# Low-part products of the last 64 gating tokens as 64-row matmul pairs

## The chip, the cores and the metric

The kernel runs on one core of one Trainium2 chip. The metric is the device time of one execution in microseconds (us); where several executions were timed, their median is given.

## The reference

Three layers follow one another: attention with rotary positions, a gated layer that mixes tokens, and a layer with a short convolution as gate. Shapes: batch 4, 8 heads of 64, 576 tokens, model width 512. The change is in the second layer:

```python
h = gelu_tanh(x @ w_in)                      # x (4, 576, 512), w_in (512, 1024)
u, v = h[..., :512], h[..., 512:]
v_n = (v - mean(v)) / sqrt(var(v) + 1e-6) * g_ln
v_s = einsum('ts,bsd->btd', w_sg, v_n) + b_sg[None, :, None]   # w_sg (576, 576)
x2  = x + (u * v_s) @ w_out
```

The sum over the 576 tokens s of `w_sg[t, s] * v_n[s, d]` is what the change touches.

## The kernel before

All matmuls outside the products with v and the sums of attention are made of parts: each number is split into a high part (rounded to a shorter type) and a low part (the rest), and a product is the sum of high x high, high x low and low x high, each a matmul in the shorter type.

In the gating, a *unit* computes 128 of the 512 features d for all 576 queries t: its accumulators are two halves of 288 queries, `ps[:, 0]` and `ps[:, 1]`, in two banks. The 576 tokens s are four chunks of 128 and a rest of 64. For the four chunks a unit runs 3 matmuls each per half of the queries (line 724). The rest has only 64 rows, so it is doubled up: a tile `T4` of 128 rows holds the high part of the 64 tokens in rows 0 to 63 and their low part in rows 64 to 127, and the chunk 4 of the weights holds the same 64 rows twice (lines 338 and 339), high parts in `SG[0]` and low parts in `SG[1]`. A matmul of the whole of `T4` with `SG[0]` therefore adds high x high and low x high; one with `SG[1]` adds high x low and low x low (line 727). So a unit is 2 x (12 + 2) = 28 matmuls, and there are four units for each of four batches.

`T4` is written by ScalarE twice from the normalized values (lines 696 and 697: the high part, into rows 64 to 127 and into rows 0 to 63), and then GpSimd subtracts the high part from the values and puts the low part into rows 64 to 127 (lines 699, 700; in the profile the tile is called `t`, and the subtraction has the line of its helper, 250).

After its last matmul VectorE reads a unit's accumulators, scales and adds the bias (line 731), GpSimd multiplies with u, and the result goes to memory. Four accumulator tiles take turns.

The order of the work on all engines is not written by hand. Each step is added to a plan with an engine, an estimated cost (`PASS` = 0.132 us a matmul of 288 columns) and the keys that it reads and writes; the plan works out due times and lays the steps out one after the other, each engine in its own queue. TensorE's steps keep the order in which they were added. A batch adds the products for v (line 671), those for u (line 710) and then the four gating units.

Other lines that are named below are of the attention stage: line 418 (scores for the maximum, two matmuls of 64 rows, one for each of two heads), line 426 (the same for the last 64 keys' queries, 128 rows), line 464 (transposed scores, four pairs of 64-row matmuls), line 472 (the rest of the keys, eight matmuls of 128 rows), line 495 (products with v, 128 rows and 64 columns). Line 789 is the first product of the last stage.

Of the kernel before, what the change touches and what calls it, by code (L numbers as in the profile page):

```python
# [26 lines left out]
class Plan:  # L27
# [6 lines left out]
    def add(self, eng, cost, fn, r=(), w=(), after=(), lat=0.0, lock=False, kb=0.0):  # L34
        k = len(self.tasks)
        deps = set(after)
        for key in r:
            deps.update(self.writer.get(key, ()))
        for key in w:
            deps.update(self.writer.get(key, ()))  # L40
            deps.update(self.readers.get(key, ()))
        for key in r:
            self.readers.setdefault(key, []).append(k)
        for key in w:
            self.writer[key] = [k]
            self.readers[key] = []
        if eng == "PE":
            if self.last_pe is not None:
                deps.add(self.last_pe)
            self.last_pe = k  # L50
        deps.discard(k)
        self.tasks.append((eng, cost, fn, tuple(sorted(deps)), lat, lock, (tuple(w) or tuple(r))[0:1]))
        self.kb.append(kb)
        return k
# [95 lines left out]
def act(n):  # L150
    return 0.11 + 0.833e-3 * n
# [15 lines left out]
def mixer_kernel(ctx: ExitStack, tc: tile.TileContext, qk, v, vrem, cs, w_in, g_ln, w_sgT, b_sg,  # L167
# [78 lines left out]
    def tt(e, out_, a, b, op, n, r, w):  # L246

        if e == "D":
            return add("DVE", dve(n), lambda: nc.vector.tensor_tensor(out_(), a(), b(), op), r, w, lock=True)  # L249
        return add("Pool", pool(n), lambda: nc.gpsimd.tensor_tensor(out_(), a(), b(), op), r, w, lock=True)  # L250
# [407 lines left out]
    def part_a(b):  # L658
        X, Wm, SG = (XH, XL), (w_h, w_l), (s_h, s_l)
        VN, T4, U, GL, VS, ST = (lambda n=n: T[n] for n in ("vn", "t4", "u", "gl", "vs", "st"))  # L660
        hl = "hl"
        xk = [("X", k, m) for k in range(4) for m in hl]
        for c0 in (0, 2, 4):
            cs_ = (c0, c0 + 1) if c0 < 4 else (4,)

            def mm(ps, cs_=cs_):
                for y, c in enumerate(cs_):
                    o = 128 * c if c < 4 else S - 128
                    for k in range(4):
                        for z, (p, q) in enumerate(three(3)):  # L670
                            nc.tensor.matmul(ps[:, y], X[p][:, k, o:o + 128], Wm[q][:, k, 512:1024], start=k == z == 0,  # L671
                                             stop=k == 3 and z == 2)
            ps, kp = unit(12 * 0.233 * len(cs_), mm, [*xk, *[(f"win{k}_1", m) for k in range(4) for m in hl]])
            gi = c0 // 2 % 2
            kg = ("gl", gi)
            n2 = len(cs_)
            add("Act", act(512 * n2), lambda ps=ps, gi=gi, n2=n2: nc.scalar.activation(
                GL()[gi][:, 0:n2], ps[:, 0:n2], AF.Gelu_apprx_tanh), [kp], [kg])
            for y, c in enumerate(cs_):
                kst = ("st", c % 3)  # L680

                def st(c=c):
                    return ST()[c % 3]
                add("DVE", dve(512), lambda st=st, gi=gi, y=y: nc.vector.bn_stats(st()[:, 0:6], GL()[gi][:, y]), [kg], [kst])
                add("DVE", 0.12, lambda st=st: nc.vector.bn_aggr(st()[:, 6:8], st()[:, 0:6]), w=[kst])
                add("DVE", 0.12, lambda st=st: nc.vector.tensor_scalar(st()[:, 8:9], st()[:, 7:8], 1e-6, None, ALU.add), w=[kst])
                add("Pool", 0.6, lambda st=st: nc.gpsimd.tensor_tensor(st()[:, 9:10], st()[:, 8:9], mhalf, ALU.pow),
                    [("consts",)], [kst])
                add("DVE", 0.46, lambda st=st, gi=gi, y=y: nc.vector.tensor_scalar(
                    GL()[gi][:, y], GL()[gi][:, y], st()[:, 6:7], st()[:, 9:10], ALU.subtract, ALU.mult), [kst, kg],  # L690
                    [("gl", gi, y)], lock=True)
                if c < 4:
                    split(lambda c=c: VN()[0][:, c], lambda c=c: VN()[1][:, c], lambda gi=gi, y=y: GL()[gi][:, y], DM,
                          [("gl", gi, y), kg], ("vn", c, "h"), ("vn", c, "l"))
                else:
                    add("Act", 2 * act(512), lambda gi=gi: (nc.scalar.copy(T4()[0][64:128], GL()[gi][64:128, 0]),
                                                            nc.scalar.copy(T4()[0][0:64], GL()[gi][64:128, 0])),
                        [("gl", gi, y), kg], [("vn", 4, "h")])
                    tt("P", lambda: T4()[0][64:128], lambda gi=gi: GL()[gi][64:128, 0], lambda: T4()[0][64:128].bitcast(F32),
                       ALU.subtract, 512, [("gl", gi, y), kg, ("vn", 4, "h")], [("vn", 4, "l")])  # L700

        def u_unit(dd):
            dc = slice(128 * dd, 128 * dd + 128)

            def mm(ps):
                for hf in range(2):
                    cols = slice(HALF * hf, HALF * hf + HALF)
                    for k in range(4):
                        for z, (p, q) in enumerate(three(3)):
                            nc.tensor.matmul(ps[:, hf, 0:HALF], Wm[p][:, k, dc], X[q][:, k, cols], start=k == z == 0,  # L710
                                             stop=k == 3 and z == 2)
            ps, kp = unit(24 * PASS, mm, [*xk, *[(f"win{k}_0", m) for k in range(4) for m in hl]])
            add("Act", act(S), lambda: nc.scalar.activation(U()[0][:, dd], ps[:, :, 0:HALF], AF.Gelu_apprx_tanh), [kp],
                [("u", dd)])

        def g_unit(dd):
            dc = slice(128 * dd, 128 * dd + 128)

            def mm(ps):
                for hf in range(2):  # L720
                    cols = slice(HALF * hf, HALF * hf + HALF)
                    for k in range(4):
                        for z, (p, q) in enumerate(three(3)):
                            nc.tensor.matmul(ps[:, hf, 0:HALF], VN()[p][:, k, dc], SG[q][:, k, cols], start=k == z == 0,  # L724
                                             stop=False)
                    for z in range(2):
                        nc.tensor.matmul(ps[:, hf, 0:HALF], T4()[0][:, dc], SG[z][:, 4, cols], start=False, stop=z == 1)  # L727
            ps, kp = unit(28 * PASS, mm, [("vn", c, m) for c in range(5) for m in hl] + [("sg", c, m) for c in range(5) for m in hl])
            y = dd % 2
            kv = ("vs", y)  # L730
            add("DVE", dve(S), lambda: nc.vector.scalar_tensor_tensor(
                VS()[y], ps[:, :, 0:HALF], gsb[:, dd:dd + 1], bsb, ALU.mult, ALU.add), [kp, ("gsb",), ("bsb",)], [kv])
            tt("P", lambda: VS()[y], lambda: VS()[y], lambda: U()[0][:, dd], ALU.mult, S, [("u", dd)], [kv])
            dma(290, lambda q: q.dma_start(out=g_d[b][dc, :], in_=VS()[y].rearrange("p a b -> p (a b)")), [kv],
                [("g_d", b, dd)])

        for dd in range(4):
            u_unit(dd)
        if b + 1 < B:
            x_prep(b + 1)  # L740
        for dd in range(4):
            g_unit(dd)
# [129 lines left out]
    def close_att():  # L872
        stT.close()
        p1 = ctx.enter_context(tc.tile_pool(name="pB1", side="right", bufs=1))
        for nm in "ovq":
            T["wh" + nm] = p1.tile([128, 4, DM], F32R, name=f"wh_{nm}")
            T["wl" + nm] = p1.tile([128, 4, DM], F32R, name=f"wl_{nm}")
        T["gh"] = [p1.tile([128, 4, S], F32R, name="gh0"), XH]
        T["gl_"] = [p1.tile([128, 4, S], F32R, name="gl0"), XL]
        pa2 = stA2.enter_context(tc.tile_pool(name="pA2", side="right", bufs=1))  # L880
        T["vn"] = [pa2.tile([128, 4, DM], F32R, name=f"vn{j}") for j in range(2)]
        T["t4"] = [pa2.tile([128, DM], F32R, name="t4")]
        T["u"] = [pa2.tile([128, 4, S], F32, name="u")]
        T["gl"] = [pa2.tile([128, 2, 512], F32, name=f"gl_{j}") for j in range(2)]
        T["vs"] = [pa2.tile([128, 2, HALF], F32, name=f"vs{j}") for j in range(2)]
        T["st"] = [pa2.tile([128, 12], F32, name=f"st{j}") for j in range(3)]
# [108 lines left out]
```

## Time and profile before

| | |
|---|---|
| median of 3 runs | 607.65 us (605.95 to 608.03) |
| profiled execution | 606.36 us |
| its span, first to last instruction | 604.6 us |
| mean granted TensorE clock | 0.986 of full |
| TensorE matmul busy | 586.5 us, 97% of the span |
| TensorE weight load (PEld) busy | 472.0 us, 78% |
| VectorE / ScalarE / GpSimd busy | 392.6 / 276.4 / 299.0 us |

In the rows of the trace PE is TensorE's matmuls and PEld its weight loads, which can overlap matmuls. An operation is written as line, operation, output<-inputs, then for TensorE the rows*columns of the array that it uses and the shape of its moving operand. Matmuls overlap in the pipeline, so the duration of one is longer than the step from its start to the start of the next. "x2" at one line joins two instructions. What stands in brackets is idle time before an instruction and what ended it; "issue" means that the engine waited for nothing that the profile shows.

### The profile page before, as it was taken

What the parts mean: (1) busy time and instruction counts of PE and PEld (TensorE: products, weight loads), DVE (VectorE), ACT (ScalarE), POOL (GpSimd) and SP (SyncE); (2) the same over time, 40 slices, a digit from 0 to 9 for tenths busy, and PEclk for the clock granted to TensorE, in tenths of its full rate; (3) what the DMA queues carried; (4) which work ended last, traced back from release to release, by engine and by line L of the source; (5) the groups of instructions that cost most, each with busy time, mean ns of one, the idle gap of its engine ahead of it and who ended that gap; (6) DMA issues with size and microseconds to landing.
All of it is one profiled execution on the core that took longest, in us unless ns stands there. A gap on an engine that the chain in (4) does not pass through costs nothing.

```text
span 604.6 us, 12082 instructions
## 1 busy us (share of the span) xinstructions
PE 586.5 (97%) x4682; PEld 472.0 (78%) x4682; DVE 392.6 (65%) x584; ACT 276.4 (46%) x448; POOL 299.0 (49%) x239
## 2 busy tenths in 40 slices
PE   7769999999999999999999999999999999999996
PEld 4546666666666666666898998998999989999995
DVE  6576777676666676654656865565397898837730
ACT  2336555556555656565542532523516454333321
POOL 5556666566555554456677846665455222201200
PEclk9679999999999999999999999999999999999999
DMA  6623555454455623666438347162433242130102
GB/s 221 205 79 91 149 165 145 126 127 126 121 128 132 188 53 91 192 192 174 139 122 298 118 149 235 47 204 91 145 116 99 60 137 92 39 127 2 36 27 95
DMA packets 55274, 76.81 MB, mean 127 GB/s; under 512 B 26544, under 2 KB 31152, under 8 KB 55216
## 3 DMA queue, kind: packets, MB, share of 16 engines
q1 hardware_dynamic: 54992, 76.03, 41.6%
q8 instruction: 37, 0.61, 0.4%
q14 instruction: 21, 0.17, 0.1%
q10 hardware_dynamic: 224, 0.00, 0.0%
HBM read 55.33 MB, written 18.95 MB: 123 GB/s over the span
## 4 chain that ended last, share of the span: by engine, by line
PE 86%; DVE 8%; issue 1%; DMA 1%; POOL 1%; ACT 0%; SPq 0%; ACTq 0%; DVEq 0%; POOLq 0%
PE ps L495 11%; PE ps L464 10%; PE ps L671 9%; PE ps L822 8%; PE ps L789 8%; PE ps L724 8%; PE ps L851 8%; PE ps L710 7%; PE ps L418 5%; DVE raw L249 4%; PE ps L472 3%; PE ps L531 3%; DVE mx L420 3%; PE ps L505 2%; PE ps L727 1%
## 5 line engine op out<-in xcount | busy, mean ns | idle before, releaser
L420 DVE TENSOR_REDUCE mx<-ps 128x2 f32<-128x576 f32 x128 | 96.4, 757 | 69.0 <-PE ps L418 68.5
L477 ACT ACTIVATE e<-ps 128x576 f32<-128x576 f32 x144 | 87.3, 649 | 77.1 <-PE ps L464 50.2
L495 PE MATMUL ps<-e,vm 128*64 128x288 f32 x512 | 78.3, 428 | 0.9 <-DVE mx L420 0.9
L250 POOL TENSOR_TENSOR ac<-e,e 128x576 f32<-128x576 f32 x32 | 50.5, 1600 | 40.3 <-PE ps L531 33.8
L724 PE MATMUL ps<-s_h,vn 128*128 128x288 f32 x256 | 56.1, 295 | 0.0
L249 DVE TENSOR_TENSOR raw<-raw,cst 128x576 f32<-128x576 f32 (+1 forms) x63 | 52.2, 857 | 6.0 <-DMA cst<-cs 6.0
L418 PE MATMUL ps<-kh,qp 64*128 64x288 f32 x256 | 49.4, 384 | 5.7 <-ACT qp L253 2.7
L418 PEld LDWEIGHTS ps<-kh,qp 64*128 64x128 f32 x256 | 25.0, 191 | 38.3 <-DVE mx L420 13.4
L250 POOL TENSOR_TENSOR raw<-raw 128x576 f32<-128x576 f32 x29 | 41.3, 1430 | 26.4 <-DVE raw L249 26.3
L495 PEld LDWEIGHTS ps<-e,vm 128*64 128x64 f32 x512 | 31.6, 138 | 24.2 <-issue 6.9
L724 PEld LDWEIGHTS ps<-s_h,vn 128*128 128x128 f32 x256 | 42.8, 188 | 0.1
L464 PE MATMUL ps<-qh,kh 64*128 64x288 f32 x256 | 41.1, 315 | 0.0
L464 PE MATMUL ps<-mr,one_r 64*128 64x288 f32 x256 | 39.3, 299 | 1.2 <-DMA mr<-mn 1.2
L464 PE MATMUL ps<-ql,kh 64*128 64x288 f32 x256 | 38.8, 297 | 0.4 <-DVE ql L249 0.4
L464 PE MATMUL ps<-qh,kl 64*128 64x288 f32 x256 | 38.6, 296 | 0.0
L822 PE MATMUL ps<-xh,wh_v 128*128 128x288 f32 x128 | 37.8, 295 | 0.0
L710 PE MATMUL ps<-XH,w_l 128*128 128x288 f32 x128 | 37.8, 295 | 0.0
L822 PE MATMUL ps<-xh,wl_v 128*128 128x288 f32 x128 | 37.8, 295 | 0.0
L724 PE MATMUL ps<-s_l,vn 128*128 128x288 f32 x128 | 37.8, 295 | 0.0
L822 PE MATMUL ps<-xl,wh_v 128*128 128x288 f32 x128 | 37.8, 295 | 0.0
L710 PE MATMUL ps<-XL,w_h 128*128 128x288 f32 x128 | 37.8, 295 | 0.0
L710 PE MATMUL ps<-XH,w_h 128*128 128x288 f32 x128 | 37.7, 295 | 0.0
(155 smaller groups left out, 1594.4 us busy)
## 6 DMA issues: line engine op xcount, KB each, us to landing
raw<-qk SPq DMA_DIRECT2D x31, 576.0 KB, 4.4
xu_d<-xu SPq DMA_DIRECT2D x32, 144.0 KB, 2.8
rb<-r_d SPq DMA_DIRECT2D x32, 144.0 KB, 3.3
xs<-xu_d SPq DMA_DIRECT2D x16, 288.0 KB, 4.0
x_d<-xs SPq DMA_DIRECT2D x16, 288.0 KB, 3.0
g_d<-vs SPq DMA_DIRECT2D x16, 288.0 KB, 3.3
vm<-v SPq DMA_DIRECT2D x16, 256.0 KB, 3.3
wr<-w_in SPq DMA_DIRECT2D x8, 512.0 KB, 5.2
```

The costliest lines, as they stand in the source:

```text
L249: return add("DVE", dve(n), lambda: nc.vector.tensor_tensor(out_(), a(), b(), op), r, w, lock=True)
L250: return add("Pool", pool(n), lambda: nc.gpsimd.tensor_tensor(out_(), a(), b(), op), r, w, lock=True)
L418: nc.tensor.matmul(ps[:, h, 0:HALF], QP[j2][rows, c], kh[rows, cols], start=True, stop=True)
L420: add("DVE", 0.76, lambda: nc.vector.tensor_reduce(out=MX[j2][:, hk, :, c], in_=ps[:, :, 0:HALF], axis=AX.X, op=ALU.max), [kps], [("mx", j ...
L464: nc.tensor.matmul(ps[:, h, 0:HALF], x[rows, keys] if o < 3 else x[rows], y[rows, cols], start=o == 0, stop=o == 3)
L477: add("Act", 0.62, lambda: nc.scalar.activation(E[n], ps[:, :, 0:HALF], AF.Exp), [kps], [("e", n)])
L495: nc.tensor.matmul(pv[64 * hf:64 * hf + 64, h, 0:HALF], VM[j2][:, j, h], E[EU[i, us[hf]]][:, h], start=j == 0, stop=False, skip_group_chec ...
L671: nc.tensor.matmul(ps[:, y], X[p][:, k, o:o + 128], Wm[q][:, k, 512:1024], start=k == z == 0, stop=k == 3 and z == 2)
L710: nc.tensor.matmul(ps[:, hf, 0:HALF], Wm[p][:, k, dc], X[q][:, k, cols], start=k == z == 0, stop=k == 3 and z == 2)
L724: nc.tensor.matmul(ps[:, hf, 0:HALF], VN()[p][:, k, dc], SG[q][:, k, cols], start=k == z == 0, stop=False)
L789: nc.tensor.matmul(ps[:, hf, 0:HALF], w2("o", p)[:, k, dc], (T["gh"], T["gl_"])[q][j][:, k, cols], start=k == z == 0, stop=k == 3 and z == 2)
L822: nc.tensor.matmul(ps[:, hf, 0:HALF], w2("v", p)[:, k, dc], (T["xh2"], T["xl2"])[q][j][:, k, cols], start=k == z == 0, stop=k == 3 and z == 2)
```

## The change

Of each unit, the matmuls of `T4` with the low parts of the weights (two, one per half of the queries, 128 rows each) are replaced by two of 64 rows: rows 0 to 63 for the first half of the queries, and rows 64 to 127 for the second half, issued one behind the other at the end of the unit. The low x low product falls away. For the second one the high part is needed in rows 64 to 127 as well, so there is a second tile `T4()[1]`: the first of the two ScalarE copies goes to its rows 64 to 127, and GpSimd's subtraction reads the high part from there and writes the low part to `T4()[0]` as before. The plan's cost of a unit is 27 passes in place of 28.

```diff
-                    add("Act", 2 * act(512), lambda gi=gi: (nc.scalar.copy(T4()[0][64:128], GL()[gi][64:128, 0]),
+                    add("Act", 2 * act(512), lambda gi=gi: (nc.scalar.copy(T4()[1][64:128], GL()[gi][64:128, 0]),
                                                             nc.scalar.copy(T4()[0][0:64], GL()[gi][64:128, 0])),
                         [("gl", gi, y), kg], [("vn", 4, "h")])
-                    tt("P", lambda: T4()[0][64:128], lambda gi=gi: GL()[gi][64:128, 0], lambda: T4()[0][64:128].bitcast(F32),
+                    tt("P", lambda: T4()[0][64:128], lambda gi=gi: GL()[gi][64:128, 0], lambda: T4()[1][64:128].bitcast(F32),
                        ALU.subtract, 512, [("gl", gi, y), kg, ("vn", 4, "h")], [("vn", 4, "l")])
...
-                    for z in range(2):
-                        nc.tensor.matmul(ps[:, hf, 0:HALF], T4()[0][:, dc], SG[z][:, 4, cols], start=False, stop=z == 1)
-            ps, kp = unit(28 * PASS, mm, [("vn", c, m) for c in range(5) for m in hl] + [("sg", c, m) for c in range(5) for m in hl])
+                    nc.tensor.matmul(ps[:, hf, 0:HALF], T4()[0][:, dc], SG[0][:, 4, cols], start=False, stop=False)
+
+                for hf in range(2):
+                    rows = slice(64 * hf, 64 * hf + 64)
+                    nc.tensor.matmul(ps[:, hf, 0:HALF], T4()[hf][rows, dc], SG[1][rows, 4, HALF * hf:HALF * hf + HALF],
+                                     start=False, stop=True)
+            ps, kp = unit(27 * PASS, mm, [("vn", c, m) for c in range(5) for m in hl] + [("sg", c, m) for c in range(5) for m in hl])
...
-        T["t4"] = [pa2.tile([128, DM], F32R, name="t4")]
+        T["t4"] = [pa2.tile([128, DM], F32R, name=f"t4_{j}") for j in range(2)]
```

## Rows read from the trace of the kernel before

**Rows 1.** The page: busy time by engine, and the chain that ended last by engine.
```profile
PE 586.5 (97%) x4682; PEld 472.0 (78%) x4682; DVE 392.6 (65%) x584; ACT 276.4 (46%) x448; POOL 299.0 (49%) x239
...
PE 86%; DVE 8%; issue 1%; DMA 1%; POOL 1%; ACT 0%; SPq 0%; ACTq 0%; DVEq 0%; POOLq 0%
```
**Rows 2.** Windows: gating units of batch 1, and the last stage; columns in the first line.
```profile
core 0: us, PE busy (x) PEld busy (x) DVE busy (x) ACT busy (x) POOL busy (x), PEclk, DMA share, GB/s
...
351.10:365.93 14.83, 14.83 (x114) 14.83 (x113) 9.43 (x11) 3.22 (x6) 9.32 (x6) 1.00 0.66 205
...
448.90:604.60 155.70, 151.10 (x985) 142.03 (x983) 103.49 (x142) 59.82 (x101) 31.59 (x18) 1.00 0.22 73
```
**Rows 3.** Chain in order of time, batch 1's gating: start, us, what.
```profile
351.10 1.60 PE ps L724 x12
352.70 0.27 PE ps L727 x2
...
365.93 0.23 PE ps L671
```
**Rows 4.** What TensorE's matmuls waited for, 311 us to the end: total, times, longest.
```profile
PE ps L727 <- POOL t L250: 0.9, 1, 0.9
```
**Rows 5.** Timeline of TensorE, end of batch 1's gating: start, us, instruction.
```profile
365.50 0.30 PE L727 MATMUL ps<-s_h,t 128*128 128x288 f32 x1
365.64 0.29 PE L727 MATMUL ps<-s_l,t 128*128 128x288 f32 x1
365.77 0.39 PE L671 MATMUL ps<-w_h,XH 128*128 128x512 f32 x1
```
**Rows 6.** Timeline of TensorE: 128 rows to 64, first and last of thirteen places.
```profile
61.02 0.29 PE L472 MATMUL ps<-mr,one_b 128*128 128x288 f32 x1
61.24 0.40 PE L418 MATMUL ps<-kh,qp 64*128 64x288 f32 x2
61.57 0.46 PE L495 MATMUL ps<-e,vm 128*64 128x288 f32 x2
...
248.74 0.29 PE L472 MATMUL ps<-mr,one_b 128*128 128x288 f32 x1
248.97 0.40 PE L418 MATMUL ps<-kh,qp 64*128 64x288 f32 x2
```
**Rows 7.** Timeline of the weight loads at another of these places.
```profile
108.08 0.19 PEld L472 LDWEIGHTS ps<-mr,one_b 128*128 128x128 f32 x1
108.44 0.19 PEld L418 LDWEIGHTS ps<-kh,qp 64*128 64x128 f32 x2 [0.16 <-issue]
```
**Rows 8.** Timeline of TensorE: 64 rows to 128.
```profile
200.24 0.40 PE L418 MATMUL ps<-kh,qp 64*128 64x288 f32 x2
200.57 0.40 PE L472 MATMUL ps<-qh,krh 128*128 128x288 f32 x1
200.81 0.30 PE L472 MATMUL ps<-qh,krl 128*128 128x288 f32 x1
```
**Rows 9.** Timeline of TensorE: a pair behind another shape, then pairs of its own.
```profile
203.28 0.40 PE L418 MATMUL ps<-kh,qp 64*128 64x288 f32 x2
203.51 0.30 PE L464 MATMUL ps<-qh,kh 64*128 64x288 f32 x2
203.65 0.29 PE L464 MATMUL ps<-qh,kl 64*128 64x288 f32 x2
```
**Rows 10.** Timeline of TensorE: line 464 to line 426.
```profile
70.68 0.29 PE L464 MATMUL ps<-mr,one_r 64*128 64x288 f32 x2
71.11 0.30 PEld L426 LDWEIGHTS ps<-kh,qr 128*128 128x128 f32 x2 [0.38 <-DVE mx L420]
```
**Rows 11.** Timeline of GpSimd before batch 0's first use of the tile.
```profile
308.07 1.48 POOL L250 TENSOR_TENSOR vn<-gl,vn 128x512 fp32r<-128x512 f32 x1
309.62 1.26 POOL L250 TENSOR_TENSOR t<-gl,t 64x512 fp32r<-64x512 f32 x1
```
**Rows 12.** Timeline of ScalarE, the copy that goes to the new tile.
```profile
308.48 0.62 ACT L696 CAST t<-gl 64x512 fp32r<-64x512 f32 x1 [2.39 <-DVE gl L689]
```

## The prediction

> **What bounds the kernel.** I read the page first, then the stretch of the gating stage by windows, then the chain of work that ended last in order of time, then what TensorE waited for from there to the end, and last TensorE's own instructions around the edited place. The page [rows 1] shows TensorE busy for 97% of the span, and 86% of the chain that ended last lying on it. The edited products are those of lines 724 and 727. The chain [rows 3] shows them back to back: twelve matmuls of line 724, two of line 727, and so on, with nothing of another engine between them, until the next batch's matmuls of line 671 follow at once. In the same stretch the windows [rows 2] show TensorE busy for 14.83 of 14.83 us at the full granted clock, and in the last stage for 151.10 of 155.70 us. From 311 us to the end the only wait of TensorE that the trace names is one of 0.9 us, the first use of the last tokens' tile in batch 0 [rows 4]. So whatever time a unit of these products gains or loses reaches the end of the program one for one: a gain isn't eaten by a wait, and a loss has no cover. The activity of VectorE, ScalarE and GpSimd only matters where it makes TensorE wait, which after 311 us is nowhere.
>
> **The price of one matmul there.** A batch holds four units of 28 matmuls, 112 in all, and takes 365.93 - 351.10 = 14.83 us [rows 3], 0.132 us each. The last ones of a batch show it singly: starts 0.13 to 0.14 us apart, the next line's matmul 0.13 us behind the last [rows 5]. Each record is 0.29 us long, but the next begins inside it; the step from start to start is the price, not the duration. Its weight load is hidden behind the matmul before.
>
> **What is removed.** Each unit has two full-height matmuls of the tile of the last 64 tokens for each half of the queries, four slots. The change keeps two and puts two 64-row matmuls, one per half of the queries, in the place of the other two. The count of instructions stays 28. If the two small ones run side by side in one slot, a unit loses one slot: 16 units x 0.132 = 2.1 us less. That two such matmuls do run side by side is in the trace: line 464 is a run of 64-row pairs of the same width and number type, listed as "x2" at one start, and the pairs stand 0.13 to 0.14 us apart [rows 9].
>
> **What is added: two changes of shape per unit.** Before, every matmul from 311 us on had 128 rows. Now each unit goes from 128 rows to 64 and back. The trace of before has both changes in the attention stage, and I price them there.
>
> Into 64 rows: line 472 (128 rows) is followed by one lone pair of line 418 (64 rows). From the last start of line 472 to the start of the pair's record it is 0.22 us (61.02 to 61.24; 248.74 to 248.97), in thirteen of thirteen such places between 60 and 276 us within 0.21 to 0.23 [rows 6]. Within one shape it would be 0.13. The pair's weight load is not late for a semaphore: it stands 0.16 us idle with "issue" as its end, so nothing that the profile sees released it [rows 7]; and the record of the pair begins together with this load, 0.40 us long in place of 0.29, so the load is in the open.
>
> Out of 64 rows: from the pair of line 418 to the first matmul of line 472 it is 0.33 us (200.24 to 200.57), again the same within 0.01 us in thirteen places, and from there to the second matmul of line 472 0.24 us (200.57 to 200.81) in place of 0.13, because its first weight load is in the open as well [rows 8]. The pair's own open load is about 0.10 of the 0.33: a pair of line 418 after another shape is followed by a pair of its own shape 0.23 us later, and that one by the next 0.14 us later [rows 9].
>
> The sum for one unit, from the start of the last full-height matmul to the start of the second matmul of what follows: after, 0.22 + 0.33 + 0.24 = 0.79 us. Before, four slots: 4 x 0.132 = 0.53 us. So a unit gets 0.26 us longer; the slot saved (0.13) is paid for by about 0.39 us of changing shape twice and of two open weight loads. Sixteen units: +4.2 us. Three of the sixteen are followed by the wider line 671 and one by line 789, all 128 rows, so the way out is the same for them.
>
> Bounds for this unknown in the place itself. From below: if the first weight load after either change were hidden after all, 0.10 less for each; with one hidden it is +0.16 us a unit, +2.6 us in all; with both hidden +0.06 a unit, +1.0 us. No row shows a hidden load behind a change, as line 418 and line 472 each have it open every time, so I hold to the full price. From above: the longest change in the trace is 0.43 us, from the pair of line 464 at 70.68 to line 426 at 71.11, against 0.33 in my sum; but there the load was held for 0.38 us by VectorE's maximum [rows 10], so it isn't a price of the change. Taken anyway it gives 0.10 x 16 = 1.6 us more, +5.8 us. I take +4.2 since the rows nearest to it (lone pair, same width, full rows on one side) say so with hardly any spread.
>
> The same can be put to rules. [Rows 9] show a pair in one slot inside a run of pairs. The Trainium skill, "TensorE: Matmul & The Clock Gate", Part 3 (packing small matmuls), says that small matmuls on different row groups run concurrently, at the time of one and some 4 ns for each further tile, and that weight loads for another row group overlap matmuls in flight; by this alone the sum is the 2.1 us saved. [Rows 6] and [rows 8] show the lone pair paying on both sides. The Trainium skill, "TensorEngine Tiling (Array Packing)", Tiling Modes, Key Properties, speaks against the change: going from one tiling mode to another drains TensorE; it gives no time for that, and with the times of those rows the sum is +4.2.
>
> **The rest of the change costs nothing.** ScalarE still makes two copies of 64 x 512 and GpSimd one subtraction of it, of the same shapes; only the tile that one copy goes to is another [rows 11, 12]. No DMA, queue entry or other instruction is added. The pair waits also for the copy into the second tile, which started at 308.48 and took 0.62 us, while the subtraction that the full-height matmul waits for anyway ran from 309.62 for 1.26 us [rows 11, 12]: the new wait is over first. The first unit's stall of 0.9 us [rows 4] therefore stays. VectorE reads the unit's accumulators after the pair in place of the last full matmul; four accumulators take turns, and TensorE waits for none of them after 311 us.
>
> The planner sees 27 passes in place of 28, so due times behind the units move by up to 16 x 0.132 = 2.1 us, and the order of loads and of work on GpSimd, ScalarE and VectorE may change somewhere, as may the addresses of the tiles that follow the new one. With TensorE at 100% this shows only near the one stall: taken away, 0.9 us gained; one GpSimd operation of 1.48 us [rows 11] put ahead of the subtraction, 1.5 us lost. I take 0 and leave it to the range.
>
> **Time.** The span is 604.6 us in an execution of 606.36 us, so 1.8 us lie around it. The three runs' median is 607.65, 1.3 above the profiled one; I set out from midway, 607.0. 607.0 + 4.2 = 611.2 us.
>
> **Rivals.**
> *The change of shape is free here.* Lines 418 and 426 stand where TensorE also waits for VectorE, and some of their gaps could be such waits that the profile doesn't name; the pair in the gating waits for nothing. Then TensorE packs the pair into one slot and 16 x 0.132 = 2.1 us go: 604.9 us, faster. Against it: thirteen equal gaps of 0.22 and thirteen of 0.33; waits for another engine would scatter. It decides once the two changes and open loads together cost under 0.13 us a unit. This is also what the Trainium skill's Part 3 of "TensorE: Matmul & The Clock Gate" taken alone would give. Chance 5%.
> *The loads are partly hidden.* The long even stream lets TensorE fetch weights ahead across the change; +1.0 to +2.6 us, 608.0 to 609.6. For it: the chain gives TensorE no other wait; against it: line 472 follows line 418 without a named wait and is open each time. Chance 12%, half of it under 0.3% (1.8 us, about what a measurement of this kernel can tell from no change).
> *The two small matmuls run one after the other*, because they close sums that full-height matmuls opened. One more slot a unit, 2.1 us more: +6.3, 613.3 us. For it no row: line 464 closes its sums in pairs too [rows 9]. Chance 5%.
> *The forecast*, both changes at full price: 78%, its own range 609.5 to 613.
>
> From these: faster 3% (most of the first), same 8% (the rest of it and half of the second), slower 89%. The range reaches over the dearer part of the hidden loads and to the serial pair: 608.6 to 613.6.
>
> **What would show it.** Right: in the profile after, the lone pair starts 0.22 us after the last full matmul with an idle weight load ended by "issue", the next unit 0.33 us later, its second matmul 0.24 after that; a batch's four units take 14.83 + 4 x 0.26 = 15.9 us; TensorE's lines around them keep their times, and no new wait is named. Wrong: four units in about 14.3 us (free change) or about 16.4 us (pair in series), or a longer stall before the first use of the last tokens' tile than 0.9 us, or a difference that lies outside these sixteen units.

## The result, and the profile after

The changed kernel took 611.18 us (median of 4 runs, 610.2 to 612.0) beside 607.15 us for the kernel before in the same session: ratio 1.0069, 95% interval 1.0051 to 1.0087. It is slower by 0.7%, or 4.0 us between the medians; 611.2 us was forecast.

Busy times of the engines, from the page of the changed kernel, which answer to the first of [rows 1]:

```profile
span 609.1 us, 12084 instructions
...
PE 590.0 (97%) x4682; PEld 471.1 (77%) x4682; DVE 391.4 (64%) x584; ACT 276.8 (45%) x448; POOL 300.3 (49%) x239
```

The same number of matmuls, 4682, and a span 4.5 us longer. The chain that ended last, in order of time, for batch 1 (start, us, what). Line 726 now is the full-height product of the last tokens, line 730 the two of 64 rows:

```profile
325.62 14.14 PE ps L671 x60
...
352.48 1.60 PE ps L724 x12
354.08 0.14 PE ps L726
354.22 1.59 PE ps L724 x12
355.80 0.13 PE ps L726
355.94 0.33 PE ps L730 x2
356.27 1.80 PE ps L724 x12
...
367.86 0.33 PE ps L730 x2
368.19 14.14 PE ps L671 x60
```

Before, this chain had twelve matmuls of line 724 in 1.60 us and two of line 727 in 0.27, all alike [rows 3]. Now the pair takes a piece of 0.33 us, the twelve matmuls behind it 1.80 us in place of 1.6, and the wider matmuls of line 671 behind the batch's last pair 14.14 us (13.94 before). From one batch's first matmul of line 671 to the next one's it is 368.19 - 325.62 = 42.57 us; before it was 365.93 - 324.44 = 41.49 us, by these lines of the chain before:

```profile
324.44 13.94 PE ps L671 x60
...
365.93 13.94 PE ps L671 x60
```

That is +1.08 us a batch, 0.27 a unit, and at that rate 4.3 us for four batches.

The windows of the stretches that [rows 2] show, with the same columns, and TensorE's waits from the gating to the end, as in [rows 4]:

```profile
352.48:368.19 15.71, 15.71 (x114) 14.49 (x112) 8.29 (x11) 3.24 (x6) 9.64 (x6) 1.00 0.60 208
...
453.29:609.10 155.81, 151.17 (x984) 142.20 (x984) 104.11 (x142) 59.91 (x100) 32.54 (x19) 1.00 0.22 72
```
```profile
PE ps L726 <- POOL t L250: 0.9, 1, 0.9
```

TensorE counts as busy for all of the 15.71 us at the full granted clock, and the weight loads for 14.49 us, where before both were busy for the whole 14.83. So the extra time shows as a hole in the row of the weight loads and not in that of the matmuls, whose recorded durations reach over it. No wait was added, and the last stage takes 155.81 us where it took 155.70. TensorE's instructions at one boundary between units, then the weight loads there:

```profile
359.49 0.29 PE L724 MATMUL ps<-s_h,vn 128*128 128x288 f32 x1
359.62 0.29 PE L726 MATMUL ps<-s_h,t 128*128 128x288 f32 x1
359.84 0.40 PE L730 MATMUL ps<-s_l,t 64*128 64x288 f32 x2
360.17 0.40 PE L724 MATMUL ps<-s_h,vn 128*128 128x288 f32 x1
360.41 0.30 PE L724 MATMUL ps<-s_l,vn 128*128 128x288 f32 x1
```
```profile
359.49 0.19 PEld L726 LDWEIGHTS ps<-s_h,t 128*128 128x128 f32 x1
359.84 0.19 PEld L730 LDWEIGHTS ps<-s_l,t 64*128 64x128 f32 x2 [0.16 <-issue]
360.17 0.19 PEld L724 LDWEIGHTS ps<-s_h,vn 128*128 128x128 f32 x1
360.27 0.19 PEld L724 LDWEIGHTS ps<-s_l,vn 128*128 128x128 f32 x1
```

From the last full-height matmul to the pair 0.22 us, from there to the next unit 0.33, to its second matmul 0.24: 0.79 us where four slots of 0.132 lay. The loads show where the time lies. In a stream of one shape a load starts while the matmul before it is still running (line 726's at 359.49, its matmul at 359.62). Line 730's load starts only at 359.84, with its matmul's record, and the next unit's first load at 360.17, again with its matmul. Only the load behind that runs ahead again (360.27 for a matmul at 360.41). Every change of shape here comes with such a load in the open; how much of the price is the change itself and how much the load, no run separates.

### The profile page after: what moved, and what is told of

Same layout as the page of the kernel before. It is cut to its first block, busy times and chain, and to the rows that moved or that the text cites. A ratio compares the mean times of both kernels' runs of the same rounds, so it can differ in the third digit from the quotient of the medians.

```text
span 609.1 us, 12084 instructions
## 1 busy us (share of the span) xinstructions
PE 590.0 (97%) x4682; PEld 471.1 (77%) x4682; DVE 391.4 (64%) x584; ACT 276.8 (45%) x448; POOL 300.3 (49%) x239
## 4 chain that ended last, share of the span: by engine, by line
PE 82%; DVE 7%; DMA 4%; POOL 2%; issue 2%; ACT 1%; SPq 1%; DVEq 0%; ACTq 0%; POOLq 0%
PE ps L464 10%; PE ps L495 10%; PE ps L724 8%; PE ps L793 8%; PE ps L826 8%; PE ps L855 8%; PE ps L671 7%; PE ps L710 6%; PE ps L418 5%; PE ps L531 4%; PE ps L472 3%; DVE raw L249 3%; DVE mx L420 2%; PE ps L505 2%; PE ps L426 1%
```

## The experiments

A *slot* is the 0.132 us from one start to the next in a stream of one shape. My theory was that the price belongs to a *visit* to 64 rows: two changes of shape, each with a weight load in the open. Its rivals were the plan's new order or the shifted tiles, a price of each 64-row matmul wherever it stands, and a pair that doesn't run side by side. All diffs are against the changed kernel. Beside the ratio I give the time from one batch's first matmul of line 671 to the next one's. All of it is TensorE's chain, with no wait, so it is free of what happens in the first 60 us, which differs from run to run (last section).

**Everything but the matmuls.**

```diff
-                    nc.tensor.matmul(ps[:, hf, 0:HALF], T4()[0][:, dc], SG[0][:, 4, cols], start=False, stop=False)
-                for hf in range(2):
...
+                    for z in range(2):
+                        nc.tensor.matmul(ps[:, hf, 0:HALF], T4()[0][:, dc], SG[z][:, 4, cols], start=False, stop=z == 1)
```

> All of the change but its matmuls: second tile, copy into it, 27 passes in the plan, with the 28 full-height matmuls of before. My theory (the price is TensorE's two changes of shape and open weight loads around each lone pair): as before, 607.2 us, ratio 1.000 within 0.002. Rival (the new order of the plan, or the shifted tiles, cost the time): 611.2 us, ratio 1.007.

Measured: 606.09 us beside 606.78, ratio 0.9991 (0.9976 to 1.0005). Its chain:

```profile
327.16 13.94 PE ps L671 x60
...
368.65 13.94 PE ps L671 x60
```

41.49 us a batch, the same as before to the last digit shown. The plan's 27 passes, the second tile and the copy into it cost nothing that shows; the cause lies in the matmuls.

**Two visits a unit.** The 64-row matmul moves into the loop over the halves, behind each half's full-height product of the last tokens.

```diff
-                for hf in range(2):
-                    rows = slice(64 * hf, 64 * hf + 64)
-                    nc.tensor.matmul(ps[:, hf, 0:HALF], T4()[hf][rows, dc], SG[1][rows, 4, HALF * hf:HALF * hf + HALF],
-                                     start=False, stop=True)
+                    rows = slice(64 * hf, 64 * hf + 64)
+                    nc.tensor.matmul(ps[:, hf, 0:HALF], T4()[hf][rows, dc], SG[1][rows, 4, cols], start=False, stop=True)
```

> The same products, but each 64-row matmul stands alone behind its own half of the queries, so that a unit changes shape four times in place of two. My theory: one visit to 64 rows adds 0.79 us from the last full start to the second one behind it, less the two slots of 0.132 that lie there anyway, 0.53 us; two visits 1.05 us a unit, less the two slots saved 0.26, so +0.79 us a unit against before, 16 units +12.6 us: 619.8 us, ratio 1.021. Rival (the price lies with the 64-row matmuls themselves, wherever they stand): as the changed kernel, 611.2 us, or with the side by side lost 2.1 us more, 613.3 us.

Measured: 620.39 us, ratio 1.0231 (1.0206 to 1.0256). TensorE at one of the lone matmuls (line 728):

```profile
357.69 0.29 PE L726 MATMUL ps<-s_h,t 128*128 128x288 f32 x1
357.92 0.40 PE L728 MATMUL ps<-s_l,t 64*128 64x288 f32 x1
358.25 0.40 PE L724 MATMUL ps<-s_h,vn 128*128 128x288 f32 x1
358.49 0.29 PE L724 MATMUL ps<-s_l,vn 128*128 128x288 f32 x1
```

A single 64-row matmul costs 0.23, 0.33 and 0.24 us, what the pair costs. A batch takes 371.80 - 327.10 = 44.70 us between these lines of its chain, 3.21 more than before (four units at +0.79, 3.16, expected):

```profile
327.10 14.20 PE ps L671 x60
...
371.80 14.20 PE ps L671 x60
```

The price goes with the visits and not with the count of 64-row matmuls.

**One visit a batch, and two.** The pairs of four units (`NV = 4`) or of two (`NV = 2`) stand together behind the first of them. They close its sums and open those of the others, and in the plan that first unit claims the others' accumulators too.

```diff
...
+                for d in range(NV if dd % NV == 0 else 0):
+                    pd = PS[(k0 + d) % 4]
+                    for hf in range(2):
+                        rows = slice(64 * hf, 64 * hf + 64)
+                        nc.tensor.matmul(pd[:, hf, 0:HALF], T4()[hf][rows, 128 * (dd + d):128 * (dd + d) + 128],
+                                         SG[1][rows, 4, HALF * hf:HALF * hf + HALF], start=d > 0, stop=d == 0)
...
```

> The same 16 pairs, but the four pairs of a batch stand together at the end of its first unit, and open the sums of the other three units: one visit a batch. My theory: a visit costs 0.53 us and three more pairs 3 x 0.132 = 0.40, together 0.92; saved are eight slots, 1.06 us; 0.13 us less a batch, 4 batches -0.5 us against before: 606.6 us, ratio 0.999, and 4.8 us less than the changed kernel. Rival (each 64-row pair has its price): 611.2 us, ratio 1.007. Third: the sums opened early wait for the accumulators of the products for u; then TensorE has a new wait before the visit.

> As the version with one visit a batch, but two: the pairs of two units stand together, behind the first of them. My theory: eight visits of 0.53 us with one more pair of 0.13 each, 0.66 us, for four slots saved, 0.53: 8 x 0.13 = +1.0 us against before, 608.0 us, ratio 1.002; between one visit a batch (0.9988 measured) and four (1.0069), closer to the first. Rival (the price is that of the last unit's evacuation or of pairs that open sums, not of visits): at the level of one visit, or at that of four.

Measured, one visit: 606.63 us beside 606.78, ratio 0.9988 (0.9971 to 1.0006). Two visits: 607.43 beside 606.95, ratio 1.0013 (1.0001 to 1.0026). TensorE at the single visit of a batch (line 733; lines 725 and 727 are the former 724 and 726), its chain (line 672 is the former 671), and what TensorE waited for from 300 to 600 us:

```profile
350.74 0.29 PE L727 MATMUL ps<-s_h,t 128*128 128x288 f32 x1
350.97 0.80 PE L733 MATMUL ps<-s_l,t 64*128 64x288 f32 x8
351.70 0.40 PE L725 MATMUL ps<-s_h,vn 128*128 128x288 f32 x1
351.93 0.30 PE L725 MATMUL ps<-s_l,vn 128*128 128x288 f32 x1
```
```profile
320.92 13.95 PE ps L672 x60
...
362.28 13.94 PE ps L672 x60
```
```profile
PE ps L727 <- POOL t L251: 0.9, 1, 0.9
```

Four pairs take 0.73 us from their start to the next shape, where one takes 0.33: 0.13 for each further pair, the price of a slot. So inside a visit two 64-row matmuls do cost one slot. A batch takes 41.36 us, 0.13 less than before, as worked out; and there is no new wait for accumulators, so the third possibility is out. With two visits it is 366.01 - 324.23 = 41.78 us, 0.29 more than before (0.26 expected), between the two levels at one of which the rival has it:

```profile
324.23 13.95 PE ps L672 x60
...
366.01 13.95 PE ps L672 x60
```

**Both 64-row matmuls on the same rows.**

```diff
-                    rows = slice(64 * hf, 64 * hf + 64)
-                    nc.tensor.matmul(ps[:, hf, 0:HALF], T4()[hf][rows, dc], SG[1][rows, 4, HALF * hf:HALF * hf + HALF],
+                    rows = slice(0, 64)
+                    nc.tensor.matmul(ps[:, hf, 0:HALF], T4()[0][rows, dc], SG[1][rows, 4, HALF * hf:HALF * hf + HALF],
```

> As the changed kernel, but both 64-row matmuls of a unit use rows 0 to 63, so that they can't run side by side; the shapes change as often. My theory: one more slot a unit, 16 x 0.132 = +2.1 us against the changed kernel: 613.3 us, ratio to before 1.0104. Rival (the pair doesn't run side by side in the changed kernel either): as the changed kernel, 611.2 us, ratio 1.007.

Measured: 613.74 us, ratio 1.0108 (1.0089 to 1.0126). TensorE at one boundary:

```profile
361.21 0.29 PE L726 MATMUL ps<-s_h,t 128*128 128x288 f32 x1
361.43 0.53 PE L730 MATMUL ps<-s_l,t 64*128 64x288 f32 x2
361.89 0.40 PE L724 MATMUL ps<-s_h,vn 128*128 128x288 f32 x1
```

0.46 us from the pair to the next shape in place of 0.33: one slot more. The side by side of the changed kernel is real and is worth 0.13 us a unit; it is only less than the visit costs.

**The low-part products left out.**

```diff
-                    nc.tensor.matmul(ps[:, hf, 0:HALF], T4()[0][:, dc], SG[0][:, 4, cols], start=False, stop=False)
-                for hf in range(2):
...
+                    nc.tensor.matmul(ps[:, hf, 0:HALF], T4()[0][:, dc], SG[0][:, 4, cols], start=False, stop=True)
```

> Leaves out the products of the last 64 tokens with the weights' low parts; a unit has 26 full-height matmuls and no change of shape. My theory: two slots a unit less than before, 32 x 0.132 = -4.2 us: 602.6 us, ratio 0.993; so the pair of the changed kernel costs 16 x 0.53 = 8.5 us in all, twice the four slots' half that it replaces. Rival (a slot in this stream isn't on the path): as before.

Measured: 602.82 us beside 606.95, ratio 0.9924 (0.9908 to 0.9941). Its chain:

```profile
324.85 13.95 PE ps L671 x60
...
365.33 13.95 PE ps L671 x60
```

40.48 us a batch: 1.01 less than before, eight slots. A slot is on the path. Against the changed kernel it is 42.57 - 40.48 = 2.09 us a batch, 0.52 us for each visit with its pair (0.53 worked out), where the two full-height matmuls that the pair stands for cost 0.25 (1.01 / 4).

The batch times side by side, in us; "worked out" uses 0.132 for a slot and 0.53 for a visit with one pair, and takes off the eight slots of before:

| | visits a batch | batch | to before | worked out |
|---|---|---|---|---|
| before | 0 | 41.49 | | |
| everything but the matmuls | 0 | 41.49 | 0.00 | 0 |
| changed | 4 | 42.57 | +1.08 | +1.06 |
| same rows | 4 | 43.09 | +1.60 | +1.59 |
| two visits a unit | 8 | 44.70 | +3.21 | +3.18 |
| two units a visit | 2 | 41.78 | +0.29 | +0.27 |
| four units a visit | 1 | 41.36 | -0.13 | -0.13 |
| left out | 0 | 40.48 | -1.01 | -1.06 |

For the row of the same rows the chain's lines are these:

```profile
327.06 14.18 PE ps L671 x60
...
370.15 14.13 PE ps L671 x60
```

## Why the prediction was right

*What bounds.* TensorE was the path from the gating to the end, and each slot won or lost there came through one for one: shown by the version with the products left out (-4.1 us in the medians for 32 slots, 4.2 by 0.132) and by the last stage, which kept its length to 0.1 us.

*The slot saved.* Right: the pair runs side by side, shown by the version on the same rows, which takes a slot more, and by the visit of four pairs.

*The two changes of shape.* Right: 0.22, 0.33 and 0.24 us were read from the attention stage's lone pairs [rows 6, 8] and came back in the gating, at the boundary shown and, within 0.01 us, at all sixteen units of that trace; only ahead of line 671 is the last step 0.33 to 0.34, on top of its wider matmuls' own 0.23. The reading of the loads held too: as in [rows 7], no load ran ahead across a change, into 64 rows or out of them. The rule of the Trainium skill that speaks against the change ("TensorEngine Tiling (Array Packing)", Tiling Modes, Key Properties: a change of tiling mode drains TensorE) agrees with the trace; the price is the runs' own, 0.79 us where 0.53 lay.

*The rest at nothing.* Right: everything but the matmuls costs 0.00 us a batch. The stall of 0.9 us at the first use of the tile stayed, and no reordering shows in the time.

*The rivals.* That the change of shape is free in a stream without waits and that loads are partly hidden are out, by the boundary shown and by the version with two visits a unit. That the pair runs in series is out by the version on the same rows, which really does so and takes a slot more.

*What was off.* Nothing that the sum rests on. As a marker I had the four units of a batch take 15.9 us, and they take 15.71 up to line 671. The price of the last way out falls into that line's first matmuls, 14.14 in place of 13.94 us; together it is 0.27 us a unit where 0.26 was worked out. And 0.43 us is not the longest change in the trace before: the same two lines are 0.65 us apart at 226.79 us, where VectorE's maximum holds the load for 0.59. I had put that change aside as a wait, so the sum doesn't hang on it; as an upper bound it would have stood 5.1 us (0.32 x 16) above the sum, outside the range.

*What was chance.* The forecast total, 611.2 us, meets the median of 611.18 more closely than the method can: the four times lie between 610.2 and 612.0, the kernel before took 607.15 where I set out from 607.0, and the medians differ by 4.0 where I had +4.2. The size is better checked in the trace. These are the first products of the last tokens, before and after, in the two chains:

```profile
310.94 0.53 PE ps L727 x2
```
```profile
311.25 0.40 PE ps L726
```

From there to the end of the span it is 604.6 - 310.94 = 293.66 us before and 609.1 - 311.25 = 297.85 after, 4.2 us more, as summed up. The other 0.3 of the span's 4.5 us lies ahead of the changed place.

Of the versions that keep the high x low products of the last tokens, none clearly beats the kernel before. The one with a single visit a batch is 0.13 us a batch shorter in its chain, 0.5 us in all, too little for the measured times to tell from no change (0.9971 to 1.0006).

## What to carry to other kernels

Packing two half-height matmuls saves one slot (0.13 us here) for each pair, but going to 64 rows and back costs 0.39 us besides, once for each visit. By these numbers a lone pair in a full-height stream loses 0.26 us, three pairs in a row come out even, and from the fourth on it pays. Measured were visits of one pair, of two and of four; three were not run. Read the price from step to step of the starts, at a place of the same trace where the shapes already change, and check in the weight-load row whether the load there runs ahead; TensorE's busy share shows none of this. Where such a change is wanted, gather the packed matmuls of several sums at one place, if their accumulators are free there.

## What was not expected

The first 60 us differ between executions by more than most of these versions do. The last matmul of line 472 in one and the same step of the attention stage starts between 57.20 and 61.93 us in the eight profiled executions. TensorE's granted clock from 20 to 60 us, in the profiled executions of the changed kernel and, second, of the version with one visit a batch:

```profile
20.00:60.00 40.00, 32.12 (x269) 21.74 (x269) 25.39 (x34) 18.44 (x30) 23.19 (x16) 0.79 0.41 114
```
```profile
20.00:60.00 40.00, 32.02 (x302) 21.74 (x304) 28.27 (x39) 19.35 (x32) 25.11 (x17) 0.96 0.46 125
```

A mean of 0.79 (between its two levels, 1.2 and 2.4 GHz) against 0.96, and in the same 40 us 269 against 302 matmuls. The second execution reached batch 1's products for v at 320.92 us, the first at 325.62, 4.7 us later. Most of that is not what the versions differ by: the matmul named above (line 473 in the second kernel) started at 57.20 us in the second and at 60.95 in the first, and the first product of the last tokens at 307.53 and 311.25 us. So the second was 3.75 us ahead at 60 us and still 3.72 ahead when the gating's changed place began; only the remaining 1.0 us comes from batch 0's units. The second's line:

```profile
307.53 0.40 PE ps L727
```

The lead goes with the higher granted clock at the start; whether the clock alone makes it, and why it differs, no run was made to show. A difference of one microsecond is better read from a stretch that repeats, as the batch here, than from the total.
